# One attention and mixer kernel: the maximum behind each power-of-two scale by one transpose instead of two small products

## The chip, the cores and the metric

The kernel runs on 1 core of one Trainium2 chip. The metric is the device time of one execution in microseconds; several executions are timed and their median is taken. Times inside the kernel come from one profiled execution.

## The reference

Inputs are q, k and v of 8 batches, 8 heads, 576 positions and 64 columns, and the weights U, V, w1, w2 of a mixer.

```python
scores = q @ k.T / 8;  scores[block(i) < block(j)] = -1e9       # blocks of 64 positions
attn = softmax(scores);  x = concat_heads(attn @ v)             # 8 x 576 x 512
u  = x + (x.T @ U @ V).T                                        # mixing over positions, rank 32
out = u + relu(u @ w1) @ w2                                     # 512 -> 2048 -> 512
```

All is f32, and the result has to hold f32 accuracy.

## The kernel before

**Arithmetic.** The FFN products run in f16. So that f16 keeps f32 accuracy, each factor is multiplied by a power of two, cast to f16 (the high part), and what the cast lost is cast as well (the low part); three f16 products stand for one f32 product. The power of two of an operand comes from its largest magnitude: `power` makes it, once for each of four parts of the first weights, once for each of two groups of later weights, and once for each of the 8 batches of u, 14 times in all. It writes two numbers into `sc`, the scale and its inverse, in every partition, because later instructions on all 128 partitions read them as a scalar of their partition.

**How `power` works.** `largest` has left one maximum for each partition and piece in `mu`. L414 reduces those to one number for each partition (`one`, 128x1). A product on PE with `one` as weights and the identity as data (L418) writes the 128 numbers as one row into a PSUM bank (1x128). VectorE takes the row's maximum (L424), clamps it (L425), and makes from its exponent bits two powers of two (L426, L430), all in one partition (`row`, 1x4). A second product (L438), with a 1x128 row filled with `by` (2.0 or 0.5, `factor`) as weights, spreads the two numbers to 128 partitions and multiplies them by `by`; L440 copies them from PSUM to `sc`. `banks_s` (names bf) are the banks for the weights' scales, `banks_a` (names ba) for the batches' scales.

**Stages.** 64 heads go through attention: scores (L1237, or L1241 and L1242 from head 14 on), the row maxima (L1255), exponentials on ScalarE (L1266), the sums and their reciprocals (L1282, L1283), the normalisation on GpSimd (L1292), transposes on PE (L1325), the product with v (L1368 or L1384) and, after every second head, the mixing (L1410 to L1461). While heads go on, the first 768 hidden columns of the FFN are done for batches that are complete (`ffn_chunk`, L661 and L686). After the last head, the other 1280 columns follow in `block_products` (L910), a scheme with 7 products of blocks instead of 8.

**`agree`.** The two halves of w2 get scales that fit each other: `limits` (L499 to L501, six instructions on 128x1) bounds the second half's scale, `ratio` (L504, L505) makes `joint`, by which `level` rescales the first half.

**The order of the work.** All instructions are tasks of `Plan`: an engine, a cost in ns, a priority, the buffers read and written. `issue` plays them through in a simulated time of its own, with an event queue, and gives each engine, whenever it is free, the ready task of lowest priority number; the order that comes out is fixed in the program. Costs are altered by up to 2% with a sequence that VARIANT sets. FFN products have priority numbers from 1e6 on, so that they are taken when no attention task is ready for PE. A task with `port=True` on VectorE and any task on GpSimd are not placed at the same time; after such a VectorE task GpSimd's next instruction also waits for it, and no GpSimd task is placed until PORT (200) ns after its end.

Of the kernel before, what the change touches and what calls it, by code (L numbers as in the profile page):

```python
# [9 lines left out]
F32 = mybir.dt.float32  # L10
F32R = mybir.dt.float32r
I32 = mybir.dt.int32
F16 = mybir.dt.float16
AF = mybir.ActivationFunctionType
ALU = mybir.AluOpType
AX = mybir.AxisListType

P = 128
# [39 lines left out]
TAIL = {"PE": 165, "DVE": 78, "ACT": 105, "POOL": 20, "SP": 0}  # L58
INTO = {"PE": 355, "DVE": 60, "ACT": 60, "POOL": 200, "SP": 60}
NEAR, DL, PORT = 130, 3000, 200  # L60
VARIANT = 4
START = {"DVE": 5750, "ACT": 2750, "POOL": 3300, "SP": 700}
COL = 0.4555
LA, MP = 900.0, 500.0
# [195 lines left out]
def _act(n, sbuf=False):  # L260
    return (93 if sbuf else 52) + 0.833 * n
# [17 lines left out]
def attention_then_mixer(  # L279
# [10 lines left out]
    nc = tc.nc  # L290
# [21 lines left out]
    def buf(pool, shape, dtype, name):  # L312
        return Buf(pool.tile(shape, dtype, name=name))

    def ring(pool, n, shape, dtype, name):
        return [buf(pool, shape, dtype, f"{name}{i}") for i in range(n)]
# [77 lines left out]
    inverse = [[Buf(iv_t[:, n, x : x + 1]) for x in range(1 + B)] for n in range(3)]  # L394
    mu_r, um_r = ([b.split(8) for b in ring(fp, 2, [P, 8], F32, x)] for x in ("mu", "um"))
    one_r = [ring(fp, 2, [P, 1], F32, f"one{x}") for x in "wu"]
    row_r = [ring(fp, 2, [1, 4], F32, f"row{x}") for x in "wu"]
    factor = {}

    def largest(src, n, buf, mu, i, prio):  # L400
# [6 lines left out]
    def power(mu, n, by, sc, prio, pool):  # L407


        one, row = (take(r[0 if pool is banks_s else 1], f"{x}{pool is banks_s}") for r, x in ((one_r, "one"), (row_r, "row")))  # L410
        ba, bb = Buf(pool=pool), Buf(pool=pool)
        add(
            "DVE", 65, prio,
            lambda: nc.vector.tensor_reduce(out=one.ap, in_=mu[:, 0:n], op=ALU.max, axis=AX.X), mu.parts[:n], [one],  # L414
        )
        add(
            "PE", 310, prio,
            lambda: nc.tensor.matmul(ba[0:1, 0:P], one.ap, factor["ident"].ap, start=True, stop=True),  # L418
            [one], [ba],
        )  # L420

        def exponent():
            x = row[0:1, 0:1]
            nc.vector.tensor_reduce(out=x, in_=ba[0:1, 0:P], op=ALU.max, axis=AX.X)  # L424
            nc.vector.tensor_scalar(out=x, in0=x, scalar1=TINY, scalar2=2.0 ** 100, op0=ALU.max, op1=ALU.min)  # L425
            nc.vector.tensor_scalar(  # L426
                out=row[0:1, 2:3].bitcast(I32), in0=x.bitcast(I32), scalar1=EXPONENT, scalar2=EXPONENT,
                op0=ALU.bitwise_and, op1=ALU.bitwise_xor,
            )
            nc.vector.tensor_scalar(  # L430
                out=row[0:1, 3:4].bitcast(I32), in0=x.bitcast(I32), scalar1=EXPONENT, scalar2=EXPONENT,
                op0=ALU.bitwise_and, op1=ALU.bitwise_and,
            )

        add("DVE", 600, prio, exponent, [ba], [row])
        add(
            "PE", 310, prio,
            lambda: nc.tensor.matmul(bb[:, 0:2], factor[by][0:1, :], row[0:1, 2:4], start=True, stop=True), [row], [bb],  # L438
        )
        add("DVE", 150, prio, lambda: nc.vector.tensor_copy(sc.ap, bb[:, 0:2]), [bb], [sc])  # L440

    def multiply(out, x, y, k, prio):
        add(
# [47 lines left out]
    def agree(prio):  # L491


        a, b, c, d = (scales[n] for n in range(4))

        def limits():
            t = joint.ap
            for x, y in ((0, 1), (1, 0)):
                nc.vector.scalar_tensor_tensor(out=t, in0=a[:, x : x + 1], scalar=0.125, in1=c[:, x : x + 1], op0=ALU.mult, op1=ALU.mult)  # L499
                nc.vector.scalar_tensor_tensor(out=t, in0=t, scalar=b[:, y : y + 1], in1=d[:, x : x + 1], op0=ALU.mult, op1=(ALU.min, ALU.max)[x])  # L500
                nc.vector.tensor_copy(d[:, x : x + 1], t)  # L501

        def ratio():
            nc.vector.scalar_tensor_tensor(out=joint.ap, in0=b[:, 0:1], scalar=2.0 ** -6, in1=d[:, 0:1], op0=ALU.mult, op1=ALU.mult)  # L504
            nc.vector.scalar_tensor_tensor(out=joint.ap, in0=joint.ap, scalar=a[:, 1:2], in1=c[:, 1:2], op0=ALU.mult, op1=ALU.mult)  # L505

        add("DVE", 1700, prio, limits, [a, b, c], [d, joint])
        add("DVE", 200, prio, ratio, [a, b, c, d], [joint])

    def level(w, bufs):  # L510

# [528 lines left out]
    ident = buf(fp, [P, P], F32, "ident")  # L1040
    factor["ident"] = ident
    make_identity(nc, ident.ap)
    for x in (2.0, 0.5):
        factor[x] = buf(fp, [1, P], F32, f"factor{x}".replace(".", "_"))
        nc.vector.memset(factor[x].ap, x)

    swap = buf(ap, [P, P], F32, "swap")
    for a in (0, 64):
        nc.vector.tensor_copy(swap[:, a : a + 64], ident[:, 64 - a : P - a])
# [158 lines left out]
    def softmax(h, tiles, pr):  # L1208

        q1, k1, q2, k2, ss, mx = (r[h % len(r)] for r in (q1_r, k1_r, q2_r, k2_r, ss_r, mx_r))  # L1210
        raw = raw_r[h % len(raw_r)]
        wide = 4 in tiles
        bank = Buf(pool=banks_w if wide else banks_f if h < 8 and 3 in tiles else Rest(banks_a))

        parts, at = [], 0
        for i in tiles:
            parts.append((i, at))
            at += P * i + 64
        side = {1: (0, T), 0: (1, T), 2: (0, T)}

        def view(i, at):
            if i == 4:
                return bank[:, :, :T]
            rows, w = P if i else 64, P * i + 64
            return bank[:rows, side[i][0], side[i][1] : side[i][1] + w] if wide else bank[:rows, at : at + w]

        def products():
            for i, at in parts:
                qs = slice(P * i + 64 - (P if i else 64), P * i + 64)
                for j in range(2 if i == 4 else 1):  # L1230
                    o = bank[:, j, :T] if i == 4 else view(i, at)
                    ks = slice(j * T, j * T + T) if i == 4 else slice(0, P * i + 64)
                    if h < FS:
                        if not i:

                            o, qs = bank[:, 1, T : T + 64] if wide else bank[:, at : at + 64], slice(0, P)
                        nc.tensor.matmul(  # L1237
                            o, raw[:, qs], raw[:, S + ks.start : S + ks.stop], start=True, stop=True
                        )
                        continue  # L1240
                    nc.tensor.matmul(o, q1[:, qs], k1[:, ks], start=True, stop=False)  # L1241
                    nc.tensor.matmul(o, q2[:, qs], k2[:, ks], start=False, stop=True)  # L1242

        ns, ms = [], []
        for i in tiles:
            ns += [T] * 4 if i == 4 else [P * i + 64] * 2
            ms += [P if i else 64] * (4 if i == 4 else 2)
        if h < FS:
            add("PE", sum(1.667 * n for n in ns) / 2 + 60 * sum(i < 2 or i == 4 for i in tiles), pr, products, [raw], [bank])
        else:  # L1250
            add("PE", _pe(*ns, m=ms) + (60 if wide else 30 + 33 * sum(i < 2 for i in tiles)), pr, products, [q1, k1, q2, k2], [bank])
        for i, at in parts:
            add(
                "DVE", _dve(P * i + 64), pr,
                lambda i=i, at=at: nc.vector.tensor_reduce(  # L1255
                    out=mx[: P if i else 64, i : i + 1], in_=view(i, at), op=ALU.max, axis=AX.XY if i == 4 else AX.X,
                    negate=True,
                ),
                [bank], [mx.parts[i]],
            )  # L1260
        for i, at in parts:
            pt, rows = pt_r[i][h % PB[i]], P if i else 64

            def exponentials(i=i, at=at, pt=pt, rows=rows):
                out = pt[:rows, : P * i + 64]
                nc.scalar.activation(  # L1266
                    out.rearrange("p (j k) -> p j k", j=2) if i == 4 else out, view(i, at), AF.Exp,
                    bias=mx[:rows, i : i + 1], accum_out=ss[:rows, i, 0:1],
                )

            add(
                "ACT", _act(P * i + 64) + 188, pr, exponentials, [bank, *(mx.parts[i] for i in tiles)],
                [pt, ss.parts[i]],
            )

# [78 lines left out]
    def apply_v(h, g, pr):  # L1354
# [6 lines left out]
        if h < FP:  # L1361
            vr, pt = vr_r[h // 2 % 2], pw_r[s][g]

            def whole_products():
                for j in range(NK[g]):

                    a, x = max(P * j - q0, 0), 5 * s + j
                    nc.tensor.matmul(  # L1368
                        bank[:, a:n], vr[:, x : x + 2, :], pt[:, _at(g, j)], start=(j == 0), stop=(j == NK[g] - 1)
                    )  # L1370

            cost = sum(5 + 1.667 * (n - max(P * j - q0, 0)) for j in range(NK[g]))
            add("PE", cost + 60, pr, whole_products, [vr, *pt.parts], [bank], hold=[xb])
            copy(False, n, pr, lambda: xt[me, q0:q1], lambda: bank[0:64, :n], [bank], [xb])
            return
        vs, tmp, ph, pl = vs_r[s], take(tmp_r, "tmp"), ph_r[g], pl_r[g]
# [177 lines left out]
```

## Time and profile before

| | us |
|---|---|
| median of 3 executions (lowest, highest) | 1133.01 (1131.96, 1133.14) |
| the profiled execution | 1132.52 |
| its span (first to last instruction) | 1130.7 |
| PE busy | 1114.4 |
| VectorE (DVE) busy | 992.4 |
| ScalarE (ACT) busy | 809.8 |
| GpSimd (POOL) busy | 495.0 |

In the profile, PE is the matmul engine and PEld its weight loads. L12 is line 12 of the kernel; names as `bf<-ident,onew` give the written and the read tiles without buffer numbers. A row of the timeline has start, length (both us), engine, line, operation, tiles, shapes and count, and in brackets the idle time of the engine before it and what ended it. A row of groups ends with the count, the busy time in us, the mean ns of one and the idle time before them. Matmuls overlap in the pipeline, so the time between starts, not their duration, tells what one takes.

### The profile page before, as it was taken

The numbers are of one execution on the slowest core, as the hardware profiler recorded it, in microseconds if no ns is written. First come the engines' busy times: TensorE is split into PE (matmuls) and PEld (weight loads), VectorE is DVE, ScalarE is ACT, GpSimd is POOL, SyncE is SP. The second block draws the span as 40 slices with busy tenths as digits, with TensorE's granted clock in tenths as the row PEclk, the third lists the DMA queues.
The fourth block names the chain that finished last, engine by engine and source line by source line (L and its number), as shares of the span: only waits on it lengthen the run. The fifth ranks groups of instructions, "written<-read, shape, count | busy, mean of one in ns | idle before, by whom it ended". The sixth has DMA issues, their size and how long they took to land.

```text
span 1130.7 us, 25478 instructions
## 1 busy us (share of the span) xinstructions
PE 1114.4 (99%) x8952; PEld 929.1 (82%) x8952; DVE 992.4 (88%) x2247; ACT 809.8 (72%) x1994; POOL 495.0 (44%) x688
## 2 busy tenths in 40 slices
PE   9999999999999999999999999999999999999998
PEld 7787788888888888888888877777777777777776
DVE  6899899999889889899899765499999899998998
ACT  7878899999889889989998854254555555454543
POOL 5334558787787777787876676000000000000000
PEclk9999999999999999999999999999999999999999
DMA  4453656554563464545543141103122130404111
GB/s 127 129 148 117 181 153 173 145 158 128 145 164 104 137 176 129 149 149 138 148 122 88 55 148 58 59 22 105 54 74 76 52 116 12 127 12 116 33 53 43
DMA packets 76720, 122.14 MB, mean 108 GB/s; under 512 B 9008, under 2 KB 53040, under 8 KB 76592
## 3 DMA queue, kind: packets, MB, share of 16 engines
q1 hardware_dynamic: 76592, 120.51, 37.3%
q8 instruction: 71, 1.16, 0.4%
q14 instruction: 57, 0.47, 0.1%
HBM read 76.23 MB, written 29.49 MB: 94 GB/s over the span
## 4 chain that ended last, share of the span: by engine, by line
PE 67%; DVE 16%; ACT 10%; issue 3%; DMA 2%; POOL 1%; SPq 0%; ACTq 0%; DVEq 0%; POOLq 0%
PE bb L910 36%; PE bf L686 8%; PE bf L661 6%; PE ba L1325 5%; ACT p L1266 4%; DVE mx L1255 4%; DVE pl L1344 3%; PE ba L1384 3%; PE ba L1368 2%; ACT ph L1302 1%; DVE xt L1392 1%; PE bw L1237 1%; DMA raw<-in_qk_dram 1%; DVE hl L669 1%; DVE ut L1445 1%
## 5 line engine op out<-in xcount | busy, mean ns | idle before, releaser
L1292 POOL TENSOR_SCALAR p<-p,rv 128x576 f32<-128x576 f32 (+4 forms) x320 | 166.2, 533 | 88.1 <-DVE rv L1283 18.3
L910 PE MATMUL bb<-ph,w2l 128*128 128x288 f16 x560 | 151.0, 286 | 0.0
L910 PE MATMUL bb<-ph,w2h 128*128 128x288 f16 x560 | 151.0, 286 | 0.0
L910 PE MATMUL bb<-ph,w1h 128*128 128x288 f16 x560 | 148.7, 286 | 0.0
L910 PE MATMUL bb<-ph,w1l 128*128 128x288 f16 x560 | 148.7, 286 | 0.0
L832 ACT CAST ph<-hb 128x576 f16<-128x576 f32 x144 | 84.3, 590 | 82.8 <-PE bb L910 77.2
L910 PEld LDWEIGHTS <-w2h 128*128 128x128 f16 x1120 | 109.6, 98 | 27.5
L910 PEld LDWEIGHTS <-w1h 128*128 128x128 f16 x1120 | 109.6, 98 | 27.5
L1325 PE MATMUL ba<-ident,p 128*128 128x128 f32 x768 | 121.4, 275 | 2.7 <-POOL p L1292 1.5
L910 PE MATMUL bb<-pl,w2h 128*128 128x288 f16 x560 | 123.5, 286 | 0.0
L1344 DVE TENSOR_TENSOR pl<-ba,ph 128x512 fp32r<-128x512 f32 x200 | 105.8, 551 | 10.1 <-ACT ph L1302 7.1
L910 PE MATMUL bb<-pl,w1h 128*128 128x288 f16 x560 | 114.4, 286 | 0.0
L686 PE MATMUL bf<-hh,w2h 128*128 128x288 f16 x384 | 110.4, 287 | 0.2 <-DVE ot L698 0.2
L686 PE MATMUL bf<-hl,w2h 128*128 128x288 f16 x384 | 109.8, 286 | 0.0
L686 PE MATMUL bf<-hh,w2l 128*128 128x288 f16 x384 | 109.8, 286 | 0.0
L1325 PEld LDWEIGHTS ba<-ident,p 128*128 128x128 f32 x768 | 89.3, 141 | 9.4 <-issue 2.9
L1302 ACT CAST ph<-ba 128x512 fp32r<-128x512 f32 x200 | 92.0, 494 | 3.5 <-PE ba L1325 2.3
L834 DVE TENSOR_TENSOR pl<-hb,ph 128x576 f16<-128x576 f32 x144 | 91.4, 655 | 1.0
L686 PEld LDWEIGHTS <-w2h 128*128 128x128 f16 x768 | 75.1, 98 | 19.7 <-issue 1.1
L1266 ACT ACTIVATE p<-ba,mx 64x64 f32<-64x64 f32 (+1 forms) x176 | 86.0, 492 | 6.2 <-DVE mx L1255 5.4
L661 PEld LDWEIGHTS <-w1h 128*128 128x128 f16 x768 | 73.9, 98 | 18.7 <-issue 1.2
L1384 PE MATMUL ba<-ph,vs 128*128 128x256 f32 (+3 forms) x400 | 84.3, 269 | 0.5 <-DVE ut L1445 0.5
(191 smaller groups left out, 3105.4 us busy)
## 6 DMA issues: line engine op xcount, KB each, us to landing
raw<-in_qk_dram SPq DMA_DIRECT2D x63, 288.0 KB, 3.9
o_d<-ot SPq DMA_DIRECT2D x72, 144.0 KB, 1.8
vr<-in_v_dram SPq DMA_DIRECT2D x32, 320.0 KB, 3.6
ur<-u_d SPq DMA_DIRECT2D x64, 144.0 KB, 2.5
wr<-o_d SPq DMA_DIRECT2D x32, 288.0 KB, 3.1
out_dram<-wr SPq DMA_DIRECT2D x31, 288.0 KB, 2.3
st<-in_w_dram SPq DMA_DIRECT2D x16, 512.0 KB, 4.3
u_d<-ut SPq DMA_DIRECT2D x28, 288.0 KB, 2.5
```

What stands on the lines that cost most here:

```text
L661: nc.tensor.matmul(ps[:, :T], w()[wn][:, k, fs], m[k].ap, start=(i == 0), stop=(i == len(ops) - 1))
L686: nc.tensor.matmul(ps[:, :T], w()[wn][:, f, ms], hs[f][x].ap, start=(i == 0), stop=(i == len(ops) - 1))
L832: add("ACT", _act(n * T, True), E, lambda: nc.scalar.copy(h.ap[:, :n, :], x[0]()), [x[1]], [h])
L834: "DVE", _dve(n * T), E, lambda: nc.vector.tensor_sub(l.ap[:, :n, :], x[0](), h.ap[:, :n, :]), [x[1], h], [l],
L910: nc.tensor.matmul(bank[:, i, :T], x()[:, w(k)], p.ap[:, k, :], start=first and n == 0, stop=last and n == len(ops) - 1)
L1255: lambda i=i, at=at: nc.vector.tensor_reduce(out=mx[: P if i else 64, i : i + 1], in_=view(i, at), op=ALU.max, axis=AX.XY if i == 4 else AX.X,
L1266: nc.scalar.activation(out.rearrange("p (j k) -> p j k", j=2) if i == 4 else out, view(i, at), AF.Exp, bias=mx[:rows, i : i + 1], accum_ou ...
L1292: lambda x=x, rows=rows, i=i: nc.gpsimd.tensor_scalar(out=x, in0=x, scalar1=rv[:rows, i : i + 1], scalar2=1.0, op0=ALU.mult, op1=ALU.mult),
L1302: add("ACT", _act(n), pr, lambda: nc.scalar.copy(out(), inp()), reads, writes)
L1325: nc.tensor.transpose(out=bank[:, a : a + P], in_=pt_r[i][h % PB[i]][:, j * P : (j + 1) * P], identity=perm.ap)
L1344: "DVE", _dve(m), pr, lambda: nc.vector.tensor_sub(pl[:, low], bank[:, :m], f32(ph[:, low])), [bank, bh], [bl]
L1384: nc.tensor.matmul(bank[0 : c.stop, a:n], vs[:, j, c], x[:, _at(g, j)], start=(i == 0), stop=(i == len(ops) - 1))
```

## The change

`power` now makes the maximum in every partition at once. `one`, read with step zero as a 128x128 block, is transposed on PE: in every partition, the bank then holds all 128 maxima. The reduction, the clamp and the exponent operations run on 128 partitions with the same number of elements for each, and a fifth VectorE instruction multiplies the two powers by `by` and writes `sc`. The second product, the copy from PSUM, the second bank and the two `factor` rows (two memsets at the start) are gone. `limits` and `ratio` become tasks with `port=True`. Some costs of the plan are other numbers, and VARIANT is 130.

```diff
-VARIANT = 4
+VARIANT = 130
...
-    row_r = [ring(fp, 2, [1, 4], F32, f"row{x}") for x in "wu"]
+    row_r = [ring(fp, 2, [P, 4], F32, f"row{x}") for x in "wu"]
...
-        ba, bb = Buf(pool=pool), Buf(pool=pool)
+        ba = Buf(pool=pool)
...
         add(
-            "PE", 310, prio,
-            lambda: nc.tensor.matmul(ba[0:1, 0:P], one.ap, factor["ident"].ap, start=True, stop=True),
+            "PE", 115, prio,
+            lambda: nc.tensor.transpose(out=ba[:, 0:P], in_=one.ap.to_broadcast([P, P]), identity=factor["ident"].ap),
             [one], [ba],
         )

         def exponent():
-            x = row[0:1, 0:1]
-            nc.vector.tensor_reduce(out=x, in_=ba[0:1, 0:P], op=ALU.max, axis=AX.X)
+            x = row[:, 0:1]
+            nc.vector.tensor_reduce(out=x, in_=ba[:, 0:P], op=ALU.max, axis=AX.X)
...
-        add("DVE", 600, prio, exponent, [ba], [row])
-        add(
-            "PE", 310, prio,
-            lambda: nc.tensor.matmul(bb[:, 0:2], factor[by][0:1, :], row[0:1, 2:4], start=True, stop=True), [row], [bb],
-        )
-        add("DVE", 150, prio, lambda: nc.vector.tensor_copy(sc.ap, bb[:, 0:2]), [bb], [sc])
+            nc.vector.tensor_scalar(out=sc.ap, in0=row[:, 2:4], scalar1=by, scalar2=1.0, op0=ALU.mult, op1=ALU.mult)
+
+        add("DVE", 720, prio, exponent, [ba], [row, sc])
...
-        add("DVE", 1700, prio, limits, [a, b, c], [d, joint])
-        add("DVE", 200, prio, ratio, [a, b, c, d], [joint])
+        add("DVE", 2000, prio, limits, [a, b, c], [d, joint], port=True)
+        add("DVE", 450, prio, ratio, [a, b, c, d], [joint], port=True)
...
-    for x in (2.0, 0.5):
-        factor[x] = buf(fp, [1, P], F32, f"factor{x}".replace(".", "_"))
-        nc.vector.memset(factor[x].ap, x)
...
-                "ACT", _act(P * i + 64) + 188, pr, exponentials, [bank, *(mx.parts[i] for i in tiles)],
+                "ACT", _act(P * i + 64) + 194, pr, exponentials, [bank, *(mx.parts[i] for i in tiles)],
...
-            add("PE", cost + 60, pr, whole_products, [vr, *pt.parts], [bank], hold=[xb])
+            add("PE", cost + 90, pr, whole_products, [vr, *pt.parts], [bank], hold=[xb])
```

The plan gives nearly every engine's queue another order. Two places matter below. The first is PE at the second weight scale (`onew`); `p` are normalised exponentials to be transposed, `spare` and `vr` the product with v, `raw` the scores. Before:

```order
L1325 MATMUL ba_95<-ident,p_1_173 128x128
L418 MATMUL bf_91<-ident,onew_111 1x128
L1325 MATMUL ba_97<-ident,p_1_169 128x128
L1325 MATMUL ba_97<-ident,p_1_171 128x128
L1325 MATMUL ba_97<-ident,p_1_173 128x128
...
L1368 MATMUL ba_95<-spare,vr_186 128x64
L438 MATMUL bf_90<-roww_115,factor_0_139 128x2
L1237 MATMUL ba_97<-raw_164 128x320
```

The same place in the change, whose later lines stand 4 to 7 lower (L1325 is L1318 there):

```order
L1318 MATMUL ba_95<-ident,p_1_169 128x128
L418 MATMUL bf_90<-ident,onew_111 128x128
L1318 MATMUL ba_98<-ident,p_0_170 128x128
L1318 MATMUL ba_98<-ident,p_0_172 128x128
L1318 MATMUL ba_98<-ident,p_0_170 128x128
```

Only one instruction of the scale is left in PE's queue, with 128x128 as its output, among other transposes. The second place is VectorE at `limits`; `mx` are row maxima of scores, `ut` and `um` belong to the mixing. Before:

```order
L440 COPY sc<-bf_90 128x2
L1457 TENSOR_REDUCE um_109<-ut_206 128x1
L1300 COPY spare<-ba_98 128x256
L499 SCALAR_TENSOR_TENSOR joint<-sc 128x1
L500 SCALAR_TENSOR_TENSOR joint<-joint,sc 128x1
L501 COPY sc<-joint 128x1
L499 SCALAR_TENSOR_TENSOR joint<-sc 128x1
L500 SCALAR_TENSOR_TENSOR joint<-joint,sc 128x1
L501 COPY sc<-joint 128x1
L1255 TENSOR_REDUCE mx_189<-bw 128x1 x2
L504 SCALAR_TENSOR_TENSOR joint<-sc 128x1
```

And in the change (L495 to L497 are the limits, L1248 the row maxima, L434 the new scaling):

```order
L434 TENSOR_SCALAR sc<-roww_115 128x2
L666 SCALAR_TENSOR_TENSOR hl<-bf_90,hh 128x288
L1293 COPY spare<-ba_97 128x256
...
L1248 TENSOR_REDUCE mx_185<-bw 128x1 x2
...
L495 SCALAR_TENSOR_TENSOR joint<-sc 128x1
L496 SCALAR_TENSOR_TENSOR joint<-joint,sc 128x1
L497 COPY sc<-joint 128x1
L495 SCALAR_TENSOR_TENSOR joint<-sc 128x1
L496 SCALAR_TENSOR_TENSOR joint<-joint,sc 128x1
L497 COPY sc<-joint 128x1
L695 SCALAR_TENSOR_TENSOR ot<-bf_91,iv,ur_119 128x288
```

The row maxima of the bank bw stood behind the limits and now stand ahead of them.

More of the change, by code (lines that the diff above doesn't have):

```diff
@@ L422, in exponent @@
         def exponent():
-            x = row[0:1, 0:1]
-            nc.vector.tensor_reduce(out=x, in_=ba[0:1, 0:P], op=ALU.max, axis=AX.X)
+            x = row[:, 0:1]
+            nc.vector.tensor_reduce(out=x, in_=ba[:, 0:P], op=ALU.max, axis=AX.X)
             nc.vector.tensor_scalar(out=x, in0=x, scalar1=TINY, scalar2=2.0 ** 100, op0=ALU.max, op1=ALU.min)
             nc.vector.tensor_scalar(
-                out=row[0:1, 2:3].bitcast(I32), in0=x.bitcast(I32), scalar1=EXPONENT, scalar2=EXPONENT,
+                out=row[:, 2:3].bitcast(I32), in0=x.bitcast(I32), scalar1=EXPONENT, scalar2=EXPONENT,
                 op0=ALU.bitwise_and, op1=ALU.bitwise_xor,
@@ L430, in exponent @@
             nc.vector.tensor_scalar(
-                out=row[0:1, 3:4].bitcast(I32), in0=x.bitcast(I32), scalar1=EXPONENT, scalar2=EXPONENT,
+                out=row[:, 3:4].bitcast(I32), in0=x.bitcast(I32), scalar1=EXPONENT, scalar2=EXPONENT,
                 op0=ALU.bitwise_and, op1=ALU.bitwise_and,
             )
-        add("DVE", 600, prio, exponent, [ba], [row])
-        add(
-            "PE", 310, prio,
-            lambda: nc.tensor.matmul(bb[:, 0:2], factor[by][0:1, :], row[0:1, 2:4], start=True, stop=True), [row], [bb],
-        )
-        add("DVE", 150, prio, lambda: nc.vector.tensor_copy(sc.ap, bb[:, 0:2]), [bb], [sc])
+            nc.vector.tensor_scalar(out=sc.ap, in0=row[:, 2:4], scalar1=by, scalar2=1.0, op0=ALU.mult, op1=ALU.mult)
+        add("DVE", 720, prio, exponent, [ba], [row, sc])
     def multiply(out, x, y, k, prio):
@@ L500, in limits @@
                 nc.vector.scalar_tensor_tensor(out=t, in0=t, scalar=b[:, y : y + 1], in1=d[:, x : x + 1], op0=ALU.mult, op1=(ALU.min, ALU.max)[x])
-                nc.vector.tensor_copy(d[:, x : x + 1], t)
+                last = nc.vector.tensor_copy(d[:, x : x + 1], t)
+            return last
         def ratio():
             nc.vector.scalar_tensor_tensor(out=joint.ap, in0=b[:, 0:1], scalar=2.0 ** -6, in1=d[:, 0:1], op0=ALU.mult, op1=ALU.mult)
-            nc.vector.scalar_tensor_tensor(out=joint.ap, in0=joint.ap, scalar=a[:, 1:2], in1=c[:, 1:2], op0=ALU.mult, op1=ALU.mult)
-        add("DVE", 1700, prio, limits, [a, b, c], [d, joint])
-        add("DVE", 200, prio, ratio, [a, b, c, d], [joint])
+            return nc.vector.scalar_tensor_tensor(out=joint.ap, in0=joint.ap, scalar=a[:, 1:2], in1=c[:, 1:2], op0=ALU.mult, op1=ALU.mult)
+        add("DVE", 2000, prio, limits, [a, b, c], [d, joint], port=True)
+        add("DVE", 450, prio, ratio, [a, b, c, d], [joint], port=True)
     def level(w, bufs):
```

## The prediction

> **What bounds the kernel now.** I read the page first, then busy time by stretch, then PE's own waits, then the chain of waits.
>
> ```profile
> span 1130.7 us, 25478 instructions
> PE 1114.4 (99%) x8952; PEld 929.1 (82%) x8952; DVE 992.4 (88%) x2247; ACT 809.8 (72%) x1994; POOL 495.0 (44%) x688
> PEclk9999999999999999999999999999999999999999
> PE 67%; DVE 16%; ACT 10%; issue 3%; DMA 2%; POOL 1%; SPq 0%; ACTq 0%; DVEq 0%; POOLq 0%
> ```
>
> The profiled execution took 1132.5 us, 1.8 us more than its span, and stands 0.5 us under the median of 1133.0. PE shows work in 1114.4 us of 1130.7, at full clock in every slice. Its matmuls overlap in the record, so I check this by rate.
>
> ```profile
> core 0: us, PE busy (x) PEld busy (x) DVE busy (x) ACT busy (x) POOL busy (x), PEclk, DMA share, GB/s
> 0.00:50.00 50.00, 47.68 (x270) 39.96 (x271) 36.79 (x125) 39.52 (x116) 25.64 (x54) 1.00 0.51 145
> 50.00:100.00 50.00, 47.68 (x293) 39.00 (x293) 46.51 (x132) 39.34 (x112) 19.60 (x37) 1.00 0.42 120
> 100.00:640.00 540.00, 532.18 (x4419) 461.76 (x4418) 487.18 (x1319) 491.94 (x1362) 404.75 (x564) 1.00 0.50 140
> 640.00:683.40 43.40, 42.99 (x354) 34.04 (x353) 27.88 (x49) 23.16 (x41) 29.56 (x24) 1.00 0.42 127
> 683.40:1130.70 447.30, 443.92 (x3624) 354.33 (x3622) 394.01 (x625) 215.88 (x367) 15.46 (x13) 1.00 0.21 62
> ...
> 683.37 2.21 PE bb L910 x18
> ...
> 723.06 404.27 PE bb L910 x3300
> ```
>
> The last two rows are pieces of the chain of waits (start, length, what). From 683 us on PE runs without a break: 404.27 us for 3300 products is 122.5 ns each, and nothing of the change lies there. Before it, PE stands still for 2.3 + 2.3 us in the first two stretches, 7.8 us (540.00 - 532.18) between 100 and 640 us, and 0.4 us after. VectorE and ScalarE are each busy some 90% of 100 to 640 us, so this stage is nearly balanced, but PE is the fullest. It also always has something else to do there: the FFN products of finished batches are issued whenever no attention product is ready, and those left over are done alone, without waits, from 640 us on. So PE time taken out before 640 us shortens that remainder, as long as no new waits come in. That is the choice on which the forecast rests.
>
> **The change part by part.** One scale is made 14 times: 6 times for weights (bank bf) and 8 times for a batch (bank ba).
>
> ```profile
> L418 PE MATMUL ba<-ident,oneu 128*1 128x128 f32 x16 | 3.0, 271 | 0.7 <-ACT k L1182 0.7
> L438 PE MATMUL ba<-rowu,factor 1*128 1x2 f32 x16 | 3.0, 256 | 0.0
> L418 PE MATMUL bf<-ident,onew 128*1 128x128 f32 x12 | 2.3, 271 | 0.0
> L438 PE MATMUL bf<-roww,factor 1*128 1x2 f32 x12 | 2.3, 256 | 0.0
> ...
> 48.67 0.38 PE L418 MATMUL bf<-ident,onew 128*1 128x128 f32 x2
> 48.98 0.51 PE L1237 MATMUL bw<-raw 128*128 128x288 f32 x1
> 50.11 0.13 DVE L430 TENSOR_SCALAR roww<-roww 1x1 int32<-1x1 int32 x1
> 52.09 0.38 PE L438 MATMUL bf<-roww,factor 1*128 1x2 f32 x2
> 52.40 0.66 PE L1325 MATMUL ba<-ident,p 128*128 128x128 f32 x4
> 52.51 0.16 DVE L440 COPY sc<-bf 128x2 f32<-128x2 f32 x1
> ```
>
> *PE, removed.* Each f32 product runs as two instructions (28 for 14). The timeline shows what a pair takes of PE's stream, from its start to the start of the next product: 48.98 - 48.67 = 0.31 us for L418 and 52.40 - 52.09 = 0.31 us for L438. Both pairs go: 14 x 0.62 = 8.7 us.
>
> *PE, added.* One transpose of 128x128 f32, the form of L1325, which occurs in long runs:
>
> ```profile
> 97.94 1.32 PE ba L1325 x12
> ...
> L1325 PE MATMUL ba<-ident,p 128*128 128x128 f32 x768 | 121.4, 275 | 2.7 <-POOL p L1292 1.5 <-DVE xt L1392 0.6 <-ACT p L1266 0.2
> ```
>
> Twelve take 1.32 us, 0.11 us each, although one shows a duration of 275 ns. Here it stands alone between other products, and its weights are read with step zero, which no row shows. Bounds: 0.11 us from the run, 0.31 us if it costs as much as one of the removed pairs. I take 0.12, near the run, since the products next to the removed pairs are the same ones that follow transposes elsewhere: 14 x 0.12 = 1.7 us. Net of PE: -7.0 us (bounds -7.1 and -4.3).
>
> The Trainium skill ("TensorE: Matmul & The Clock Gate", Part 4: PE-mode transpose) gives about 275 ns for a transpose in a kernel's context and says that it does not count as PE busy in the usual way. The trace has the same 275 ns as the mean duration, but the run above starts one every 0.11 us; by the page's figure as a price the PE term would be 8.7 - 3.9 = -4.8 us.
>
> *VectorE.* The maximum, the clamp and the two exponent operations stay, on 128 partitions instead of one; one more scaling takes the place of the copy from PSUM.
>
> ```profile
> L424 DVE TENSOR_REDUCE rowu<-ba 1x1 f32<-1x128 f32 x8 | 2.2, 272 | 0.3 <-PE ba L418 0.3
> L414 DVE TENSOR_REDUCE oneu<-um 128x1 f32<-128x4 f32 (+1 forms) x8 | 1.1, 141 | 0.0
> L425 DVE TENSOR_SCALAR rowu<-rowu 1x1 f32<-1x1 f32 x8 | 1.1, 142 | 0.3
> L440 DVE COPY sc<-ba 128x2 f32<-128x2 f32 x8 | 1.2, 145 | 0.1
> ```
>
> A tiny operation takes 141 ns over 128 partitions (L414) and 142 over one (L425): the partitions cost nothing, and the fifth operation costs what the copy did. I put this at zero; it lies in a stage where VectorE has 53 us of room. What does change is latency: now the scale is there 52.67 - 48.67 = 4.0 us after the first product starts, because the second product waits in PE's queue; without it, the scaling follows the exponent operations (ending at 50.24) and is done at about 50.4. That is some 2 us earlier, 14 times. Nothing on PE is seen to wait for it, so I count zero, with up to half of the 4.6 us that PE stands still in the first 100 us as the bound below.
>
> *The joint limits (L499 to L505), once.* They now exclude GpSimd.
>
> ```profile
> 133.68 0.54 DVE L499 SCALAR_TENSOR_TENSOR joint<-sc 128x1 f32<-128x1 f32 x1
> 134.26 0.79 DVE L500 SCALAR_TENSOR_TENSOR joint<-joint,sc 128x1 f32<-128x1 f32 x1
> 134.99 1.40 POOL L1183 TENSOR_TENSOR q<-raw,q 64x576 fp32r<-64x576 f32 x1
> 135.27 1.14 DVE L499 SCALAR_TENSOR_TENSOR joint<-sc 128x1 f32<-128x1 f32 x1
> 136.35 1.42 POOL L1184 TENSOR_TENSOR k<-raw,k 64x576 fp32r<-64x576 f32 x1
> 136.45 1.34 DVE L500 SCALAR_TENSOR_TENSOR joint<-joint,sc 128x1 f32<-128x1 f32 x1
> 137.89 1.01 DVE L1255 TENSOR_REDUCE mx<-bw 128x1 f32<-128x576 f32 x2
> 138.82 0.15 DVE L504 SCALAR_TENSOR_TENSOR joint<-sc 128x1 f32<-128x1 f32 x1
> 138.94 0.74 ACT L1266 ACTIVATE p<-bw,mx 128x576 f32<-128x576 f32 x1 [1.38 <-DVE mx L1255]
> 140.27 0.37 PE L1241 MATMUL bw<-k,q 128*128 128x288 f32 x1 [1.13 <-issue]
> ```
>
> The same operation takes 0.15 us at 138.82, when GpSimd is still, and 0.54 to 1.34 us while GpSimd runs. So the six take 4.1 us in place of about 1. Behind them the maximum of a softmax bank (bw) is queued, then its exponential, and PE waits 1.13 us for that bank. In the new order the maxima of bw stand ahead of the limits and the limits are short: I take the whole 1.1 us away (bounds 0 and 1.1). GpSimd stands still meanwhile; behind it wait the normalised p and then the transposes. It has 135 us of room in 100 to 640 us, so I count nothing; uncovered, it costs about what PE's longest wait for it does, 1.3 us:
>
> ```profile
> PE ba L1325 <- POOL p L1292: 1.7, 3, 1.3
> ```
>
> The Trainium skill ("SBUF — State Buffer", SBUF: two separate sides) calls the port that VectorE and GpSimd share an exclusive lock, held for a whole instruction. The rows agree: 1.14 us is a 0.15 us operation plus a wait inside the 1.40 us one of GpSimd; it changes no term.
>
> *The order.* The altered costs and VARIANT rearrange all queues; the work itself is the same. I count zero, with waits on both sides below.
>
> Sum: -7.0 - 1.1 = -8.1 us. The span would be 1122.6, the profiled execution 1124.4, the median 1133.0 - 8.1 = **1124.9 us**.
>
> **The rivals.** *Swallowed:* VectorE and ScalarE at 90% bind the stage, and PE's gain becomes waits. For it: before 683.4 us the chain of waits runs on PE only for 0.67 x 1130.7 - 447.3 = 310 us, 45%. Against it: PE has FFN products to fill with. Then 45% of 7.0 counts, 3.2, with 1.1 for the limits: 1128.7 us.
>
> *A lone transpose holds PE for its shown 275 ns:* 14 x 0.275 = 3.9 us added, net -4.8 - 1.1: 1127.1 us; this is the Trainium skill's figure of Part 4 above. Against it stands the run of twelve.
>
> *A better order:* half of the 7.8 us of standstill between 100 and 640 us goes too: 1121.0 us. Nothing in the profile speaks for or against it.
>
> *Slower: the new order makes PE wait between 100 and 640 us.* VectorE and ScalarE have 10% of room, so an order that puts a maximum or an exponential late is felt at once. If PE stood still as in 50 to 100 us (2.32 of 50.00), that is 25.1 us in 540 in place of 7.8: +17.3 - 8.1, 1142.2 us. From 15.9 us of standstill there the change loses.
>
> **How the numbers follow.** Forecast 0.60, swallowed 0.16, lone transpose 0.07, better order 0.08, slower order 0.09. 0.2% of 1133.0, 2.3 us, is about what a measurement of this kernel can tell from no change: faster is below 1130.7, slower above 1135.3. Faster: 0.57 of the forecast, 0.13, 0.06 and 0.08 of the next three, 0.84. Within: 0.03 + 0.03 + 0.01 + 0.02 of the slower order cut short, 0.09. Slower: 0.07. The range goes from the better order less 1 us, 1120, past the swallowed gain to 1131.5, and leaves out about 2 in 10. The forecast's own part is 1122 to 1128.
>
> **What would show it.** In the changed profile, 14 instructions of PE at L418, one 128x128 f32 each, whose following product starts 0.11 to 0.14 us later; no 1x2 products; the scaled exponents about 2 us after the transpose. The six limits within about 1.2 us. The stretch of pure L910 products as long as before, but beginning about 8 us earlier, and PE's standstill between 100 and 640 us near 7 us. If PE loses the 28 pairs and that stretch does not move, the gain was swallowed or the order waits; the standstill tells which. The forecast is wrong if the time lies above 1128 or below 1122.

## The result, and the profile after

The changed kernel takes 1126.33 us (median of 4 executions, 1125.78 to 1126.37) against 1133.06 us for the kernel before beside it; the ratio is 0.9942, with a 95% interval of 0.9925 to 0.9959. That is 6.7 us less; 8.1 were forecast (1124.9). The size was right to 1.4 us. The experiments will show that the main reason given for it was not.

The page and the busy time by stretch of the changed kernel, and the last two pieces of its chain of waits; the lines of the code stand 3 to 7 lower than before (L910 is L907, L1325 is L1318, L440 is L434):

```profile
span 1124.5 us, 25323 instructions
PE 1105.9 (98%) x8910; PEld 925.1 (82%) x8910; DVE 989.5 (88%) x2245; ACT 810.1 (72%) x1994; POOL 496.0 (44%) x688
PE 58%; ACT 15%; DVE 11%; issue 3%; DMA 2%; POOL 1%; SPq 0%; ACTq 0%; POOLq 0%; DVEq 0%
...
50.00:100.00 50.00, 47.37 (x286) 39.02 (x285) 45.75 (x131) 43.44 (x123) 19.06 (x37) 1.00 0.44 120
100.00:640.00 540.00, 530.78 (x4434) 462.43 (x4433) 488.88 (x1321) 491.21 (x1358) 409.12 (x564) 1.00 0.51 141
640.00:683.40 43.40, 42.31 (x349) 33.71 (x347) 26.09 (x48) 22.52 (x41) 26.47 (x24) 1.00 0.39 117
...
707.29 8.82 PE bf L683 x72
716.11 405.00 PE bb L907 x3306
```

The unbroken run of L907 products begins at 716.11 us in place of 723.06 and is as long as before. So the gain lies ahead of it, as forecast. PE is busy 8.5 us less, but it stands still 9.2 us (540.00 - 530.78) between 100 and 640 us, where it was 7.8. The chain of waits runs over ScalarE more and over PE less.

The parts of the change, in the timeline around the last scale, which is made for the last batch:

```profile
657.77 2.62 POOL L760 TENSOR_TENSOR w1l<-wr,w1h 128x1280 f16<-128x1280 f32 x1
658.48 0.27 PE L418 MATMUL ba<-ident,oneu 128*128 128x128 f32 x1
658.59 0.65 PE L658 MATMUL bf<-uh,w1h 128*128 128x288 f16 x4
659.55 0.86 DVE L434 TENSOR_SCALAR sc<-rowu 128x2 f32<-128x2 f32 x1
660.33 0.44 DVE L666 SCALAR_TENSOR_TENSOR hl<-bf,hh 128x288 f16<-128x288 f32 x1
660.82 0.65 PE L658 MATMUL bf<-uh,w1h 128*128 128x288 f16 x4 [0.60 <-DVE hl L666]
...
L434 DVE TENSOR_SCALAR sc<-rowu 128x2 f32<-128x2 f32 x8 | 3.2, 406 | 0.3
L434 DVE TENSOR_SCALAR sc<-roww 128x2 f32<-128x2 f32 x6 | 2.1, 351 | 0.2
```

The transpose takes 0.11 us of PE's stream (658.59 - 658.48). The new scaling, L434, takes 0.35 to 0.41 us on average where the copy from PSUM took 0.15: it runs from SBUF to SBUF, takes 0.17 us when GpSimd is still, and here ends when GpSimd's operation ends (657.77 + 2.62 = 660.39 us). Behind it on VectorE stands L666, and PE waits 0.60 us for that.

The six limits (L495 to L497) now take 1.5 us, from 129.85 to 131.39, in place of 4.1:

```profile
128.89 1.40 POOL L1177 TENSOR_TENSOR k<-raw,k 64x576 fp32r<-64x576 f32 x1
...
129.85 0.46 DVE L495 SCALAR_TENSOR_TENSOR joint<-sc 128x1 f32<-128x1 f32 x1
130.79 0.16 DVE L495 SCALAR_TENSOR_TENSOR joint<-sc 128x1 f32<-128x1 f32 x1
131.24 0.15 DVE L497 COPY sc<-joint 128x1 f32<-128x1 f32 x1
```

Only the first of them still meets an operation of GpSimd, which ends at 130.29.

### The profile page after: what moved, and what is told of

It reads as the page before. It is cut to its first block, busy times and chain, and to the rows that moved or that the text cites. A ratio compares the mean times of both kernels' runs of the same rounds, so it can differ in the third digit from the quotient of the medians.

```text
span 1124.5 us, 25323 instructions
## 1 busy us (share of the span) xinstructions
PE 1105.9 (98%) x8910; PEld 925.1 (82%) x8910; DVE 989.5 (88%) x2245; ACT 810.1 (72%) x1994; POOL 496.0 (44%) x688
## 4 chain that ended last, share of the span: by engine, by line
PE 58%; ACT 15%; DVE 11%; issue 3%; DMA 2%; POOL 1%; SPq 0%; ACTq 0%; POOLq 0%; DVEq 0%
PE bb L907 37%; PE bf L658 7%; PE bf L683 5%; ACT p L1259 5%; PE ba L1318 3%; DVE pl L1337 3%; PE ba L1377 2%; DVE mx L1248 2%; ACT ph L1295 2%; DMA raw<-in_qk_dram 1%; ACT tmp L1383 1%; ACT raw L1173 1%; ACT q L1170 1%; DVE xt L1385 1%; DVE ot L695 1%
## 5 line engine op out<-in xcount | busy, mean ns | idle before, releaser
L1285 POOL TENSOR_SCALAR p<-p,rv 128x576 f32<-128x576 f32 (+4 forms) x320 | 169.2, 544 | 92.9 <-DVE rv L1276 21.1
L907 PE MATMUL bb<-ph,w2h 128*128 128x288 f16 x560 | 151.0, 286 | 0.0
L907 PE MATMUL bb<-ph,w2l 128*128 128x288 f16 x560 | 151.0, 286 | 0.0
L907 PE MATMUL bb<-ph,w1h 128*128 128x288 f16 x560 | 148.7, 286 | 0.0
L907 PE MATMUL bb<-ph,w1l 128*128 128x288 f16 x560 | 148.7, 286 | 0.0
L907 PEld LDWEIGHTS <-w2h 128*128 128x128 f16 x1120 | 109.6, 98 | 27.5
L907 PEld LDWEIGHTS <-w1h 128*128 128x128 f16 x1120 | 109.6, 98 | 27.5
L1318 PE MATMUL ba<-ident,p 128*128 128x128 f32 x768 | 121.6, 274 | 3.9 <-POOL p L1285 1.2
L907 PE MATMUL bb<-pl,w2h 128*128 128x288 f16 x560 | 123.5, 286 | 0.0
L907 PE MATMUL bb<-pl,w1h 128*128 128x288 f16 x560 | 114.4, 286 | 0.0
L1318 PEld LDWEIGHTS ba<-ident,p 128*128 128x128 f32 x768 | 89.8, 141 | 9.4 <-POOL p L1285 2.9
```

Of the source, the lines that this page charges most:

```text
L907: nc.tensor.matmul(bank[:, i, :T], x()[:, w(k)], p.ap[:, k, :], start=first and n == 0, stop=last and n == len(ops) - 1)
L1285: lambda x=x, rows=rows, i=i: nc.gpsimd.tensor_scalar(out=x, in0=x, scalar1=rv[:rows, i : i + 1], scalar2=1.0, op0=ALU.mult, op1=ALU.mult),
L1318: nc.tensor.transpose(out=bank[:, a : a + P], in_=pt_r[i][h % PB[i]][:, j * P : (j + 1) * P], identity=perm.ap)
```

## The experiments

Theory A is the prediction's: PE's stream sets the time, so PE time taken out counts in full. Theory B is its rival: VectorE and ScalarE bind, and some 45% counts. Theory C came up after the first four runs: the order of every queue is fixed in the program, so each engine waits at fixed places for the others and for transfers, and a cut on one engine is for the most part given back at the next such place. Theory D, put beside it in two runs: one of VectorE and ScalarE binds alone. The kernel before was timed beside each kernel (medians 1132.3 to 1132.7 us); the ratios refer to it.

### The new contents in the old order

```diff
 (kernel before; the tasks of power and their costs stay)
-            lambda: nc.tensor.matmul(ba[0:1, 0:P], one.ap, factor["ident"].ap, ...
+            lambda: nc.tensor.transpose(out=ba[:, 0:P], in_=one.ap.to_broadcast([P, P]), ...
...
-            lambda: nc.tensor.matmul(bb[:, 0:2], factor[by][0:1, :], row[0:1, 2:4], ...
+            lambda: None, [row], [bb],
...
-        add("DVE", 150, prio, lambda: nc.vector.tensor_copy(sc.ap, bb[:, 0:2]), [bb], [sc])
+        add("DVE", 150, prio, lambda: nc.vector.tensor_scalar(out=sc.ap, in0=row[:, 2:4], scalar1=by, ...
```

> Edit: the kernel before, with its order kept row for row; only what power issues is new (the transpose in place of the first product, nothing in place of the second, the scaling in place of the copy from PSUM). The limits are as before. Theory A (PE's stream sets the time, so PE time that is taken out before the pure FFN stage counts in full): 28 pairs of 0.31 us go, 14 transposes of 0.11 us come, -7.1 us; in the trace of before the instruction ahead of each pair also takes 0.20 us where 0.11 is usual, and if that goes too, 28 x 0.09 = 2.6 us more, -9.7 us. Theory B (VectorE and ScalarE bind the attention stage, 45% of PE's gain counts): -3 to -4.4 us. The scaling, in SBUF from SBUF on 128x2, takes 0.15 us alone and up to 1 us while GpSimd runs.

Measured: 1133.41 us, ratio 1.0009 (1.0001 to 1.0018). Nothing is gained. The products are gone from PE all the same; its page and stretch:

```profile
PE 1108.5 (98%) x8910; PEld 925.2 (82%) x8910; DVE 995.3 (88%) x2247; ACT 809.1 (72%) x1994; POOL 494.5 (44%) x688
...
100.00:640.00 540.00, 526.59 (x4374) 457.55 (x4373) 488.20 (x1318) 490.07 (x1362) 403.50 (x561) 1.00 0.50 140
```

PE is busy 5.9 us less, and between 100 and 640 us it stands still 13.4 us, against 7.8: the time came back as waits. For this order theory A falls, and theory B's 3 us are not there either. One place where it came back, again at the scaling (L440 here):

```profile
186.44 1.42 POOL L1183 TENSOR_TENSOR q<-raw,q 64x576 fp32r<-64x576 f32 x1
186.56 1.32 DVE L440 TENSOR_SCALAR sc<-rowu 128x2 f32<-128x2 f32 x1
187.91 0.48 DVE L1392 TENSOR_TENSOR xt<-ba,tmp 64x320 f32<-64x320 f32 x1
188.45 0.66 PE L1410 MATMUL ba<-ident,xt 128*128 128x128 f32 x4 [0.82 <-DVE xt L1392]
```

In the kernel before, PE has no wait there, and the same products start at 188.57 us. The scores ahead of them start at 185.93 us here and at 187.07 before: a lead of 1.1 us shrinks to 0.1.

### The same, with the scaling as two operations on 128x1

```diff
-        lambda: nc.vector.tensor_scalar(out=sc.ap, in0=row[:, 2:4], scalar1=by, ...
+        lambda: [nc.vector.tensor_scalar(out=sc[:, i : i + 1], in0=row[:, 2 + i : 3 + i], scalar1=by, ...) for i in range(2)]
```

> Edit: fixed_order with the scaling as two operations on 128x1 in place of one on 128x2. In fixed_order the one on 128x2 took 0.14 to 1.32 us. If its waits for GpSimd's port ate PE's gain (theory A saved), the time falls from fixed_order's 1133.4 towards 1124 to 1127. Theory C (with the order fixed, each engine's queue waits for the others, and a cut on PE is given back as waits): within 2 us of fixed_order, and the two operations take 0.15 us each, without the spread.

Measured: 1132.84 us, ratio 1.0005 (0.9997 to 1.0014): theory C. The wait above is gone, and in its trace this kernel is ahead of the kernel before up to 508 us, by as much as 2.7 us; then it meets a transfer. ScalarE's timeline, first of this kernel, then of the kernel before:

```profile
506.88 0.58 ACT L1416 CAST xh<-ba 128x512 fp32r<-128x512 f32 x1 [0.24 <-PE ba L1413]
508.98 0.67 ACT L376 ACTIVATE z<-st 128x512 f32<-128x512 f32 x1 [1.51 <-DMA st<-in_w_dram]
```

```profile
508.79 0.59 ACT L1413 CAST xh<-ba 128x512 fp32r<-128x512 f32 x1 [0.27 <-PE ba L1410]
510.01 0.68 ACT L376 ACTIVATE z<-st 128x512 f32<-128x512 f32 x1 [0.64 <-DMA st<-in_w_dram]
```

It is ahead by 1.9 us at the cast and by 1.0 us after the weights' transfer, for which ScalarE waits 1.51 us in place of 0.64. About half of the lead is lost at that wait, and in the medians nothing is left of it.

### The removed products back into the changed kernel

```diff
+        def products():
+            nc.tensor.matmul(ba[0:1, 0:P], one.ap, factor["ident"].ap, start=True, stop=True)
+            nc.tensor.matmul(ba[:, 0:2], factor["ident"][0:1, :], factor["ident"][0:1, 0:2], start=True, stop=True)
+            return nc.tensor.transpose(...)
```

> Edit: the changed kernel, with its order kept, and ahead of each of the 14 transposes both removed f32 products on PE again (one with the 128x1 column as weights into a row, one with a 1x128 row as weights and two columns); the transpose then overwrites their bank. Against the changed kernel (1126.3): theory A +14 x (0.62 + about 0.09 to 0.18) = +10 to +11 us, so above 1136, slower than the kernel before, since only the order and the limits are then left of the change. Theory B: 45%, +4.5 to +5 us, 1131.

Measured: 1128.69 us, ratio 0.9961 (0.9949 to 0.9972). The ratios of this kernel and of the changed one differ by 0.0019, give or take 0.0021, which is 2.2 us (-0.2 to 4.5). The timeline shows that PE did get the work:

```profile
176.05 0.38 PE L417 MATMUL ba<-ident,oneu 128*1 128x128 f32 x2
176.36 0.38 PE L418 MATMUL ba<-ident 1*128 1x2 f32 x2
176.67 0.32 PE L419 MATMUL ba<-ident,oneu 128*128 128x128 f32 x1
176.83 0.41 PE L662 MATMUL bf<-uh,w1l 128*128 128x288 f16 x2
...
100.00:640.00 540.00, 534.22 (x4455) 464.21 (x4454) 485.99 (x1318) 489.51 (x1354) 409.23 (x564) 1.00 0.50 140
```

From the first product to the one behind the transpose are 0.78 us in place of 0.11, and the product ahead takes 0.22 us in place of 0.12 (the last section comes back to that): 14 x 0.76 = 10.6 us more on PE. Some 2 us of it reach the end; theory A's 10 us are excluded, theory B's 4.5 lie at the edge. PE stands still 5.8 us in place of 9.2. Again a transfer takes part of it. ScalarE in the changed kernel, then in this one:

```profile
237.81 0.48 ACT L376 ACTIVATE z<-st 128x320 f32<-128x320 f32 x1 [2.97 <-DMA st<-in_w_dram]
```

```profile
237.96 0.49 ACT L376 ACTIVATE z<-st 128x320 f32<-128x320 f32 x1 [1.04 <-DMA st<-in_w_dram]
```

Both go on at 237.8 to 238.0 us: this kernel came there 2 us later, and waited 1.9 us less.

### Other orders

The first two kernels are the one before with another VARIANT, the next two the changed one; the last has two costs of the plan as before.

```diff
-VARIANT = 4
+VARIANT = 130            # before_v130; 7 in before_v7
...
-VARIANT = 130
+VARIANT = 4              # after_v4; 7 in after_v7
...
-_act(P * i + 64) + 194    cost + 90      (after_oldcosts)
+_act(P * i + 64) + 188    cost + 60
```

> Edit: the kernel before with VARIANT 130 alone: the same work in another order. Theory A with an order that is worth little: within 3 us of 1133. Rival (the gain came from the new order): about 1127.

> Edit: the kernel before with VARIANT 7, a third order of the same work. If the change is worth some 2 to 3 us on average over orders and an order some 2 us either way, 1132 to 1136, above the changed kernel in the same variant (1131.4). If the change is worth nothing on average and orders alone scatter, it may lie below 1131.

> Edit: the changed kernel with VARIANT 4. Theory A: 1126 give or take 3 us, since the PE work is the same as in the changed kernel. Rival (the gain came from VARIANT): about 1133.

> Edit: the changed kernel with VARIANT 7, a third order of the same work. Orders so far: before 1132.4 (4) and 1135.1 (130), changed 1126.3 (130) and 1132.1 (4). If the change is worth some 4.5 us by itself and an order some 3 us either way: 1126 to 1132. If 1126.3 is only a lucky order and the change is worth nothing: 1131 to 1137.

> Edit: the changed kernel with two costs of the plan as before (188 in place of 194 for an exponential, 60 in place of 90 for the product with v), VARIANT 130 kept; the work is the same, the order another. If the changed kernel's 1126.3 is one lucky draw among orders: 1129 to 1134, as its variants 4 and 7. If VARIANT 130 or the new power makes orders good in general: 1125 to 1128.

| order | kernel before: us, ratio | changed kernel: us, ratio |
|---|---|---|
| VARIANT 4 | the reference, 1 | 1132.14, 0.9997 (0.9989 to 1.0005) |
| VARIANT 130 | 1135.05, 1.0023 (1.0015 to 1.0032) | 1126.33, 0.9942 (0.9925 to 0.9959) |
| VARIANT 7 | 1139.45, 1.0054 (1.0042 to 1.0067) | 1131.40, 0.9996 (0.9987 to 1.0005) |
| 130, two costs as before | | 1135.27, 1.0018 (1.0009 to 1.0027) |

The order alone moves the kernel before by 0.54%, nearly as much as the whole result (0.58%), and the changed one by 0.76%, which is more. Two cost numbers of the plan, which change no work, are worth 8.6 us. VARIANT 130 is not good in itself: it makes the kernel before slower. The 1126.3 us is the best of four draws; how VARIANT 130 was chosen for the change is not on record. Two draws, before_v7 and after_oldcosts, came out above every range given for them, so orders scatter more than was assumed. The mean of the three ratios before is 1.0026 and of the four after 0.9988, a difference of 0.4% with a standard error of 0.2% from their scatter; the draws overlap. This hints that the change is worth some 4 us on average over orders, but so few orders don't settle it.

The trace of after_v4 shows one place where this order loses time, at the last scale:

```profile
660.37 5.18 POOL L760 TENSOR_TENSOR w1l<-wr,w1h 128x1280 f16<-128x1280 f32 x2
663.22 2.35 DVE L434 TENSOR_SCALAR sc<-rowu 128x2 f32<-128x2 f32 x1
665.98 1.00 PE L658 MATMUL bf<-uh,w1h 128*128 128x288 f16 x4 [2.09 <-DVE hl L666]
...
663.00:667.00 4.00, 1.91 (x13) 1.24 (x11) 3.40 (x7) 0.41 (x1) 3.02 (x2) 0.89 0.74 196
667.00:671.00 4.00, 4.00 (x24) 2.79 (x23) 0.46 (x1) 1.38 (x4) 0.97 (x3) 0.68 1.01 320
```

The scaling met a 2.6 us operation of GpSimd, PE stood still 2.09 us, and the granted clock was 0.89 and 0.68 in the two stretches of 4 us around and behind it. That is not all of the loss: five of the twelve executions of after_v4 show a mean clock of 1.0 and not of 0.998, and their median is 1130.8 us, still 4.5 more than the changed kernel takes.

### Less on VectorE, less on ScalarE, and no limits, in the old order

```diff
-                lambda i=i, at=at: nc.vector.tensor_reduce(out=mx[...        (dve_less; mx[:, 0] is set to 0)
+                lambda i=i, at=at: i and nc.vector.tensor_reduce(out=mx[...
...
-                    bias=mx[:rows, i : i + 1], accum_out=ss[:rows, i, 0:1],    (act_less)
+                    bias=mx[:rows, i : i + 1], **({"accum_out": ss[:rows, i, 0:1]} if i else {}),
...
-        add("DVE", 1700, prio, limits, [a, b, c], [d, joint])                (no_limits)
+        add("DVE", 1700, prio, lambda: None, [a, b, c], [d, joint])
```

> Edit: the kernel before, order kept; the 64 row maxima of the first query block (64x64, 0.20 us each, 13.0 us of VectorE) are left out and zero is subtracted instead, which the softmax divides out again. Theory C, with a cut counted by the engine's share of the chain of waits before 683 us (VectorE 16% of 1131 us of 683 us, 26%): -3.4 us. Theory D (one vector engine binds): near 0 if it is ScalarE, near -10 if it is VectorE. Theory A: 0.

> Edit: the kernel before, order kept; the exponentials of the first query block (64x64) don't sum up their rows, which leaves out 64 reads of the accumulator on ScalarE (0.20 us each, 12.8 us), and those rows are divided by a constant instead of their sums. Theory C (ScalarE 10% of 1131 us of 683 us, 17%): -2.2 us. Theory D with ScalarE as the one that binds: near -10 us. Theory A: 0.

> Edit: the kernel before, order kept, with the six operations of limits left out (the second half's scale isn't bounded; ratio still makes the halves agree). The prediction's second term, taken whole: PE's wait of 1.13 us for the bank bw at 140 us goes and the time falls by 1.1 us. Theory C (what one engine gains is given back at the next wait for another): PE's wait at 140 us goes, but the time changes by less than 0.5 us.

| left out | busy time less (the page) | time, ratio |
|---|---|---|
| 64 maxima on VectorE | 6.7 us (992.4 to 985.7) | 1131.82 us, 0.9996 (0.9987 to 1.0005) |
| 64 reads on ScalarE | 6.0 us (809.8 to 803.8) | 1129.24 us, 0.9972 (0.9962 to 0.9983) |
| the six limits | 4.1 us in one place | 1130.99 us, 0.9985 (0.9977 to 0.9994) |

Busy time falls by half of what the durations add up to, since such short operations overlap with their neighbours. VectorE's 6.7 us are worth nothing that can be told from zero (at most 1.5), so theory C's count by the share of the chain, 3.4 us, is wrong there; ScalarE's 6.0 us are worth 3.2 (1.9 to 4.3), and the 2.2 of that count lie within. Theory D's 10 us, scaled to the busy time that really went, would be 5.2 for VectorE, which is excluded, and 4.7 for ScalarE, a little above the interval: ScalarE's queue comes nearest to binding. In act_less too a transfer takes part of the gain: in its trace ScalarE is 3.5 us ahead at 467 us, waits 1.33 us for weights, and is 2.0 us ahead behind them. The limits are worth 1.7 us (0.7 to 2.6), and the prediction's 1.1 lies within; theory C's bound of 0.5 does not. The bank bw's product on PE, at 140.27 with a wait of 1.13 before, follows without one:

```profile
138.94 0.29 PE L686 MATMUL bf<-hl,w2h 128*128 128x288 f16 x1
138.97 0.39 PE L1241 MATMUL bw<-k,q 128*128 128x288 f32 x1
```

So theory C is no law: here ScalarE (1.38 us) and then PE (1.13 us) both waited for VectorE, and what is cut ahead of such a place does count.

### The changed kernel with the scaling in two operations

```diff
-            nc.vector.tensor_scalar(out=sc.ap, in0=row[:, 2:4], scalar1=by, scalar2=1.0, op0=ALU.mult, op1=ALU.mult)
+            for i in range(2):
+                nc.vector.tensor_scalar(out=sc[:, i : i + 1], in0=row[:, 2 + i : 3 + i], scalar1=by, ...)
```

> Edit: the changed kernel, order kept, with the scaling as two operations on 128x1 in place of one on 128x2, which took 0.17 to 0.99 us while GpSimd ran (mean 0.38 us over 14). The two take about 0.15 us each without the spread; 14 x 0.1 us of VectorE at most. Theory C: within 1 us of the changed kernel, 1125.5 to 1127. Rival (the waits at the port lie on the path, as at 659.5 us, where PE then waits 0.6 us): -1 to -3 us.

Measured: 1122.94 us, ratio 0.9916 (0.9902 to 0.9929), below both kernels. Against the changed kernel that is 0.26%, give or take 0.22%: 2.9 us, on the side of the rival (0.5 to 5.4). The same edit was worth nothing in the old order (fixed_order 1.0009, fixed_split 1.0005).

```profile
L435 DVE TENSOR_SCALAR sc<-rowu 128x1 f32<-128x1 f32 x16 | 1.7, 149 | 0.0
L435 DVE TENSOR_SCALAR sc<-roww 128x1 f32<-128x1 f32 x12 | 1.3, 149 | 0.0
...
235.11 0.49 ACT L376 ACTIVATE z<-st 128x320 f32<-128x320 f32 x1 [1.11 <-DMA st<-in_w_dram]
...
650.97 5.19 POOL L763 TENSOR_TENSOR w1l<-wr,w1h 128x1280 f16<-128x1280 f32 x2
655.25 0.22 DVE L435 TENSOR_SCALAR sc<-rowu 128x1 f32<-128x1 f32 x2
655.38 0.45 DVE L669 SCALAR_TENSOR_TENSOR hl<-bf,hh 128x288 f16<-128x288 f32 x1
655.88 0.65 PE L661 MATMUL bf<-uh,w1h 128*128 128x288 f16 x4
```

Two operations take 0.22 us together in the midst of GpSimd's work, and PE's products run on at 655.88 without the 0.60 us of before. A second wait of PE behind the scaling, in the changed kernel, is gone as well:

```profile
419.30 0.73 DVE L434 TENSOR_SCALAR sc<-rowu 128x2 f32<-128x2 f32 x1
420.60 0.66 PE L1403 MATMUL ba<-ident,xt 128*128 128x128 f32 x4 [0.57 <-DVE xt L1385]
```

These two come to 1.2 us. The two profiled executions differ by 4.9 us (spans 1124.5 and 1119.6), and the largest step of that, 1.9 us, lies at the weights' transfer shown above, for which ScalarE waited 1.11 us and not 2.97; 0.5 us more arise in the first 13 us, before any scale is made. Whether the step at the transfer follows from the edit or is chance of that execution isn't shown, so only some 1 us of the 2.9 is traced to the scaling.

## Why the prediction was right in size and wrong in its main reason

**What bounds the kernel: wrong.** The step that failed is the sentence that PE "always has something else to do", the FFN products being "issued whenever no attention product is ready". That holds in the plan's own time, while the order is made. On the chip PE's queue is fixed: if the next product isn't ready, PE waits, though FFN products stand further back. fixed_order took 28 x 0.40 - 14 x 0.11 = 9.7 us out of PE (the 0.40 is explained below) and gained nothing; pairs_back added 10.6 us and lost about 2 (-0.2 to 4.5). Both keep an order; how much of the saving a plan made anew around it keeps is open. The changed kernel's own trace had a sign of it: PE's standstill between 100 and 640 us was 9.2 us, where near 7 was expected. PE at 99% was misread too: a product shows 0.29 us and takes 0.12 of the stream, so short waits are hidden in "busy"; of the 9.7 us only 5.9 showed as less busy time.

**PE removed and added: right as prices.** The pairs went, and 14 transposes of 0.11 us came (0.12 taken). The rival of a lone transpose at its shown 275 ns falls. The sum of -7.0 us was even too small, since the product ahead of a pair gets faster too; what failed is that it was booked in full. The Trainium skill ("TensorE: Matmul & The Clock Gate", Part 4: PE-mode transpose) gives about 275 ns for a transpose; the trace agrees with that as a duration (0.27 us at 658.48) and not as a price for the stream (0.11).

**VectorE at zero: wrong.** The four operations that stay did cost on 128 partitions what they had on one (the clamp 0.15 us, 0.14 before). But the scaling was priced by the copy from PSUM, 0.145 us; it measured 0.38 us on average and up to 2.35 (after_v4). With two operations in its place the time came down by another 2.9 us, some 1 of them traced to the scaling. It waits for GpSimd: on 128x2 it took 0.14 to 0.17 us when GpSimd was still and otherwise ended with GpSimd's operation, and on 128x1 it never waited (0.149 on average). The prediction saw such a wait at the limits and did not ask for it at the new operation. The Trainium skill ("SBUF — State Buffer", SBUF: two separate sides) says that an operation of VectorE in a two-port mode, or with two SBUF inputs, and one of GpSimd shut each other out, and that the later one waits until the other is over. The rows on 128x2 show such a wait, with the ends 0.02 to 0.05 us behind GpSimd's.

**The limits: right.** 1.1 us was the term; no_limits, which takes all six out of the old order, gave 1.7 (0.7 to 2.6). In the new order the term isn't measured by itself.

**The order at zero: wrong, and the largest term.** It moved the same work by 0.5 to 0.8%. The forecast was met by luck: a good draw (VARIANT 130 with the new costs) gave about what PE's savings had been booked for. As a rough split, not measured as a sum: of the 6.7 us, about 2 are PE's products (pairs_back), about 1 to 2 the limits by the run in the old order, and the rest is the order; what the change is worth on average over orders is open. "Swallowed" (1128.7 us, chance 0.16) was the rival nearest to the mechanism: PE's gain became waits. Its 45% were too much in the old order and at the edge in the new one, and VectorE, which it named beside ScalarE, gave nothing when relieved.

## What to carry to other kernels

Where a program fixes the order of every queue, a saving on the busiest engine can be given back as waits. If the plan is made anew around it, one timing of one order says little: draw several orders of both versions before a gain under 1% is put down to an edit. A high busy share of the matmul engine doesn't prove that it binds; take the work out with the order kept, and see. A tiny operation from SBUF to SBUF on VectorE can be priced by what GpSimd does at that moment: look at its longest durations, and not at the mean of another operation of that size.

## What the runs showed of the hardware that was not expected

A product of f32 that runs as two instructions costs more than its own 0.31 us: the product ahead of it also gives way later. In the kernel before:

```profile
48.47 0.27 PE L1325 MATMUL ba<-ident,p 128*128 128x128 f32 x1
48.67 0.38 PE L418 MATMUL bf<-ident,onew 128*1 128x128 f32 x2
```

The transpose ahead takes 0.20 us of the stream where 0.11 is usual (0.11 again in fixed_order at the same place), and most of the 28 pairs show the same 0.09: 0.40 us for a pair that writes one row of 128 numbers, or two numbers in each partition.

A multiplication on 128x2 f32 in SBUF waits for GpSimd and one on 128x1 doesn't, so that two are faster than one: 0.22 us together against 0.38 on average.

And in the one trace in which PE stood still for 2.09 us, after_v4 at 664 us, the mean granted clock fell to 0.68 behind it. In the changed kernel it did not after 1.97 us:

```profile
239.48 0.40 PE L1234 MATMUL bw<-k,q 128*128 128x288 f32 x1 [1.97 <-ACT p L1259]
...
239.00:243.00 4.00, 3.52 (x28) 3.17 (x28) 3.08 (x9) 3.49 (x12) 1.49 (x2) 1.00 0.15 17
```
